# A linear-attention block: denominators and reciprocals per block of rows, placed between the later Q blocks

## The chip, the cores and the metric

One core of a Trainium2 chip (trn2). The metric is the device time of one execution in microseconds (us), median of several runs. Each trace is one profiled execution. A run is called slow when it is over 1.5% above the fastest run of the same kernel.

Terms: TensorE does the matmuls and leaves their results in buffers of PSUM; VectorE and ScalarE read them there, and a buffer is free for the next matmul only when they have. The clock is the share of its full rate that TensorE was granted, as the profile records it; where it falls below 1.00 I say that it is cut.

## The reference, cut to what matters

```python
B, S, D = 1, 2048, 640                      # H = 32 heads of 20
q, k, v = split(x @ wqkv)                   # per head
pq, pk = phi(q), phi(k)                     # phi(t) = (t + 1 if t > 0 else exp(t)) + 1e-6
kv  = einsum("bhsd,bhse->bhde", pk, v)      # needs all rows of k and v
z   = einsum("bhsd->bhd", pk)
num = einsum("bhqd,bhde->bhqe", pq, kv)
den = einsum("bhqd,bhd->bhq", pq, z)[..., None] + 1e-6
out = (num / den) reshaped to (B, S, D) @ wo
```

The kernel folds `kv` and `wo` into one 640 x 640 matrix `gw`, so that each row of output is (pq x 1/den) @ gw. The 2048 rows go in four blocks of 512.

## The kernel before: the parts in question

```python
psum  = tile_pool("ps_main", bufs=5)   # tag "pp": five PSUM buffers for nearly everything
ps_pd = tile_pool("ps_pd", bufs=1)     # the denominator alone
ps128 = tile_pool("ps_128", bufs=2)    # transposes

setup_masks(); q_block(0)
for st in range(16): kv_tile(st)
for sb in (1, 2, 3): q_block(sb, act_relu=True)     # exp, relu on ScalarE; add on VectorE
# ... KV sums: 5 bands of 16 matmuls into g (masked kv) and zspad (z in four shifted copies)

pd = ps_pd.tile([P, 512])                           # 4 blocks x 32 heads = 128 rows
for qq in range(4):
    for k in range(5): matmul(pd, lhsT=zspad[:, k, qq], rhs=pq[:, k, block qq], ...)
nc.vector.reciprocal(rden, pd)                      # one, 128 x 512
# ... 13 transposes of g (copied out by ScalarE), 26 fold matmuls -> gw

for qq in range(4):                                 # expansion of 1/den and multiply
    for mi in range(5):
        pr = psum.tile(tag="pp")
        matmul(pr, lhsT=epad[:, qq, mi], rhs=rden)
        nc.vector.tensor_tensor(pqs[:, mi, block qq], pq[:, mi, block qq], pr, mult)
for st in range(16):                                # output
    po0, po1 = psum.tile(), psum.tile()
    # ... 5 + 5 matmuls of pqs with gw; ScalarE casts po0, VectorE casts po1, then the store
```

Of the kernel before, what the change touches and what calls it, by code (L numbers as in the profile page):

```python
# [13 lines left out]
def kernel(  # L14
# [7 lines left out]
    nc = tc.nc  # L22
    P = nc.NUM_PARTITIONS
    B, S, D = x.shape
    assert B == 1
    H = 32
    Dh = D // H
    KT = D // P
    assert D == P * KT and H * Dh == D
    NS = S // P  # L30
    SB = 512
    NSB = S // SB
    NQ = S // 512
    assert S % 512 == 0 and NQ <= 4

    bf16 = mybir.dt.bfloat16
    f32 = mybir.dt.float32
# [15 lines left out]
    bands = []  # L53
    for mi in range(KT):
        hlo = (mi * P) // Dh
        hhi = (mi * P + P - 1) // Dh
        c0 = hlo * Dh
        c1 = (hhi + 1) * Dh
# [18 lines left out]
    gt_pairs = []  # L77
    pair_idx = {}
    for kt in range(KT):
        hlo, hhi, c0, c1, _, _, _ = bands[kt]  # L80
# [5 lines left out]
    work = ctx.enter_context(tc.tile_pool(name="work", bufs=3))  # L86
# [3 lines left out]
    wo_sb = consts.tile([P, KT, D], bf16, name="wo_sb")  # L90
# [4 lines left out]
    ident = consts.tile([P, P], bf16, name="ident")  # L95
# [4 lines left out]
    g = consts.tile([P, KT, D], bf16, name="gmat")  # L100
    gt = consts.tile([P, len(gt_pairs), P], bf16, name="gtmat")
    zspad = consts.tile([P, KT, NQ, P], bf16, name="zspad")
    gw = consts.tile([P, KT, D], bf16, name="gw")
# [11 lines left out]
    for oc in ONE_COLS:  # L115
# [5 lines left out]
        out=ident[:],  # L121
        in_=ident[:],
# [6 lines left out]
    for qq in range(NQ):  # L129
        nc.gpsimd.memset(epad[:, qq, :], 1.0)  # L130
        nc.gpsimd.affine_select(
            out=epad[:, qq, :],
            in_=epad[:, qq, :],
# [7 lines left out]
            out=epad[:, qq, :],  # L141
            in_=epad[:, qq, :],
# [8 lines left out]

    with ExitStack() as p1:
        psum = p1.enter_context(tc.tile_pool(name="ps_main", bufs=5, space=bass.MemoryType.PSUM))
        ps_pd = p1.enter_context(tc.tile_pool(name="ps_pd", bufs=1, space=bass.MemoryType.PSUM))
        ps128 = p1.enter_context(tc.tile_pool(name="ps_128", bufs=2, space=bass.MemoryType.PSUM))

        def setup_masks():
# [12 lines left out]
        def evict_q(pt, out_ap):  # L170
            e = work.tile([P, 512], bf16, name="phi_e")
            r = work.tile([P, 512], bf16, name="phi_r")
            nc.scalar.activation(out=e[:, :], in_=pt[:, :], func=AF.Exp)
            nc.vector.tensor_scalar(
                out=r[:, :], in0=pt[:, :], scalar1=0.0, scalar2=EPS, op0=ALU.max, op1=ALU.add
            )
            nc.vector.scalar_tensor_tensor(
                out=out_ap, in0=e[:, :], scalar=1.0, in1=r[:, :], op0=ALU.min, op1=ALU.add
            )

        def evict_q_act(pt, out_ap):
            e = work.tile([P, 512], bf16, name="phi_e")
            r = work.tile([P, 512], bf16, name="phi_r")
            nc.scalar.activation(out=e[:, :], in_=pt[:, :], func=AF.Exp)  # L184
            nc.scalar.activation(out=r[:, :], in_=pt[:, :], func=AF.Relu, bias=epst[:], scale=1.0)  # L185
            nc.vector.scalar_tensor_tensor(  # L186
                out=out_ap, in0=e[:, :], scalar=1.0, in1=r[:, :], op0=ALU.min, op1=ALU.add
            )

        def q_block(sb, act_relu=False):  # L190
            for mi in range(KT):
                pt = psum.tile([P, 512], f32, name="pp", tag="pp")
                for k in range(KT):
                    nc.tensor.matmul(  # L194
                        pt[:, :],
                        lhsT=w_sb[:, k, bass.ts(mi, P)],
                        rhs=xt[:, k, bass.ts(sb, SB)],
                        start=(k == 0),
                        stop=(k == KT - 1),
                    )  # L200
                if act_relu:
                    evict_q_act(pt, pq[:, mi, bass.ts(sb, SB)])
                else:
                    evict_q(pt, pq[:, mi, bass.ts(sb, SB)])
# [56 lines left out]
        q_block(0)  # L261
        for st in range(NS):
            kv_tile(st)
        for sb in range(1, NSB):
            q_block(sb, act_relu=True)

        for mi in range(KT):
            hlo, hhi, c0, c1, b0, b1, zcol = bands[mi]
            W = b1 - b0
            pb = psum.tile([P, 512], f32, name="pp", tag="pp")  # L270
            for st in range(NS):
                nc.tensor.matmul(  # L272
                    pb[:, 0:W],
                    lhsT=pk[:, st, bass.ts(mi, P)],
                    rhs=va[:, st, b0:b1],
                    start=(st == 0),
                    stop=(st == NS - 1),
# [8 lines left out]
            for s0_, s1_ in segs:  # L286
# [3 lines left out]
                    out=g[:, mi, s0_:s1_],  # L290
# [6 lines left out]
                out=zspad[:, mi, 0, 0:H], in0=et[:, mi, :], scalar1=pb[:, zoff : zoff + 1]  # L297
# [1 line left out]
            for qq in range(1, NQ):  # L299
                nc.scalar.copy(out=zspad[:, mi, qq, 32 * qq : 32 * qq + H], in_=zspad[:, mi, 0, 0:H])  # L300

        pd = ps_pd.tile([P, 512], f32, name="pd", tag="pd")
        for qq in range(NQ):
            for k in range(KT):
                nc.tensor.matmul(  # L305
                    pd[:, :],
                    lhsT=zspad[:, k, qq, :],
                    rhs=pq[:, k, qq * 512 : (qq + 1) * 512],
                    start=(qq == 0 and k == 0),
                    stop=(qq == NQ - 1 and k == KT - 1),  # L310
                )
        rden = work.tile([P, 512], bf16, name="rden", bufs=1)
        npd = NQ * 32
        if npd < P:
            nc.vector.memzero(rden[:])
        with nc.allow_low_precision("bf16 reciprocal of den is fine"):
            nc.vector.reciprocal(rden[:npd, :], pd[:npd, :])

        for pi, (kt, nt) in enumerate(gt_pairs):
            ptp = ps128.tile([P, P], bf16, name="ptp", tag="t128")  # L320
            nc.tensor.transpose(ptp[:, :], g[:, kt, bass.ts(nt, P)], ident[:, :])
            nc.scalar.copy(out=gt[:, pi, :], in_=ptp[:, :])

        for kt in range(KT):
            hlo, hhi, c0, c1, _, _, _ = bands[kt]
            nts = list(range(c0 // P, (c1 - 1) // P + 1))
            HD = D // 2
            gw0 = psum.tile([P, 512], f32, name="pp", tag="pp")
            gw1 = psum.tile([P, 512], f32, name="pp", tag="pp")
            for i, nt in enumerate(nts):  # L330
                nc.tensor.matmul(  # L331
                    gw0[:, :HD],
                    lhsT=gt[:, pair_idx[(kt, nt)], :],
                    rhs=wo_sb[:, nt, 0:HD],
                    start=(i == 0),
                    stop=(i == len(nts) - 1),
                )
                nc.tensor.matmul(  # L338
                    gw1[:, :HD],
                    lhsT=gt[:, pair_idx[(kt, nt)], :],  # L340
                    rhs=wo_sb[:, nt, HD:D],
                    start=(i == 0),
                    stop=(i == len(nts) - 1),
                )
            nc.scalar.copy(out=gw[:, kt, 0:HD], in_=gw0[:, :HD])
            nc.vector.tensor_copy(out=gw[:, kt, HD:D], in_=gw1[:, :HD])

        for qq in range(NQ):
            for mi in range(KT):
                pr = psum.tile([P, 512], f32, name="pp", tag="pp")  # L350
                nc.tensor.matmul(  # L351
                    pr[:, :],
                    lhsT=epad[:, qq, bass.ts(mi, P)],
                    rhs=rden[:, :],
                    start=True,
                    stop=True,
                )
                nc.vector.tensor_tensor(  # L358
                    out=pqs[:, mi, qq * 512 : (qq + 1) * 512],
                    in0=pq[:, mi, qq * 512 : (qq + 1) * 512],  # L360
                    in1=pr[:, :],
                    op=ALU.mult,
                )

        HD = D // 2
        for st in range(NS):
            po0 = psum.tile([P, 512], f32, name="pp", tag="pp")
            po1 = psum.tile([P, 512], f32, name="pp", tag="pp")
            for k in range(KT):
                nc.tensor.matmul(  # L370
                    po0[:, :HD],
                    lhsT=pqs[:, k, bass.ts(st, P)],
                    rhs=gw[:, k, 0:HD],
                    start=(k == 0),
                    stop=(k == KT - 1),
                )
                nc.tensor.matmul(  # L377
                    po1[:, :HD],
                    lhsT=pqs[:, k, bass.ts(st, P)],
                    rhs=gw[:, k, HD:D],  # L380
                    start=(k == 0),
                    stop=(k == KT - 1),
                )
            ob = work.tile([P, D], bf16, name="ob")
            nc.scalar.copy(out=ob[:, 0:HD], in_=po0[:, :HD])  # L385
            nc.vector.tensor_copy(out=ob[:, HD:D], in_=po1[:, :HD])  # L386
            nc.sync.dma_start(out2[bass.ts(st, P), :], ob[:, :])


# [28 lines left out]
```

## Time and profile before

| | before |
|---|---|
| median at the prediction | 130.36 us (6 runs) |
| span of the profiled execution | 127.5 us |
| K/V stage ends | 60.2 us |
| last output matmul ends | 124.1 us |
| between the two ("the stretch") | 63.9 us |
| TensorE's own work in the stretch | 56.7 us |

The change touches only the stretch. I read its ends from TensorE's instructions in order of time: the end of the last K/V matmul and the end of the last output matmul. It doesn't depend on how fast the inputs arrived. The prediction shows the lines.

### The profile page before, as it was taken

What the parts mean: (1) busy time and instruction counts of PE and PEld (TensorE: products, weight loads), DVE (VectorE), ACT (ScalarE), POOL (GpSimd) and SP (SyncE); (2) the same over time, 40 slices, a digit from 0 to 9 for tenths busy, and PEclk for the clock granted to TensorE, in tenths of its full rate; (3) what the DMA queues carried; (4) which work ended last, traced back from release to release, by engine and by line L of the source; (5) the groups of instructions that cost most, each with busy time, mean ns of one, the idle gap of its engine ahead of it and who ended that gap; (6) DMA issues with size and microseconds to landing.
All of it is one profiled execution on the core that took longest, in us unless ns stands there. A gap on an engine that the chain in (4) does not pass through costs nothing.

```text
span 127.5 us, 1909 instructions
## 1 busy us (share of the span) xinstructions
PE 117.0 (92%) x674; PEld 63.1 (49%) x674; DVE 71.0 (56%) x133; ACT 66.5 (52%) x212; POOL 8.4 (7%) x18
## 2 busy tenths in 40 slices
PE   0769999999999999999999999999968999999990
PEld 0414445455445555455444449746511267777760
DVE  5306984444555554444666667409899964334331
ACT  4556355566666655566999996408500013233230
POOL 8980000000000000000000000000000000000000
PEclk9999999999999999999999999999996579999999
DMA  2989999900000000000000000000000004223422
GB/s 54 247 268 343 343 209 194 198 3 0 0 0 0 0 3 5 0 0 0 0 0 3 5 0 0 0 0 5 0 0 0 0 0 149 108 105 114 147 105 101
DMA packets 14776, 8.63 MB, mean 68 GB/s; under 512 B 10800, under 2 KB 14128, under 8 KB 14768
## 3 DMA queue, kind: packets, MB, share of 16 engines
q1 hardware_dynamic: 14768, 8.52, 23.9%
q8 instruction: 5, 0.08, 0.3%
q14 instruction: 3, 0.02, 0.1%
HBM read 3.28 MB, written 2.62 MB: 46 GB/s over the span
## 4 chain that ended last, share of the span: by engine, by line
PE 82%; DVE 5%; SPq 4%; DMA 3%; ACT 2%; issue 2%; DVEq 0%; ACTq 0%
PE pp L194 16%; PE pp L211 12%; PE pp L218 12%; PE pp L370 9%; PE pp L377 9%; PE pp L225 8%; PE pp L272 4%; DVE pqs L358 4%; PE pp L351 4%; PE pd L305 3%; DMA wqkv_sb<-in_wqkv_dram 3%; SPq L107 2%; PE pp L338 1%; SPq L109 1%; PE pp L331 1%
## 5 line engine op out<-in xcount | busy, mean ns | idle before, releaser
L211 PE MATMUL pp<-wqkv_sb,xt 128*128 128x512 bf16 x80 | 30.3, 379 | 0.0
L218 PE MATMUL pp<-wqkv_sb,xt 128*128 128x512 bf16 x80 | 30.3, 379 | 0.0
L194 PE MATMUL pp<-xt,wqkv_sb 128*128 128x512 bf16 x100 | 22.9, 385 | 1.0 <-DMA wqkv_sb<-in_wqkv_dram 1.0
L235 DVE TENSOR_SCALAR phi_r<-pp 128x512 bf16<-128x512 f32 x16 | 11.1, 692 | 21.2 <-ACT phi_e L234 21.2
L370 PE MATMUL pp<-gw,pqs 128*128 128x320 bf16 x80 | 21.9, 309 | 0.0
L377 PE MATMUL pp<-gw,pqs 128*128 128x320 bf16 x80 | 21.6, 305 | 0.0
L385 ACT CAST ob<-pp 128x320 bf16<-128x320 f32 x16 | 6.8, 426 | 26.2 <-PE pp L370 24.8
L225 PE MATMUL pp<-wqkv_sb,xt 128*128 128x256 bf16 x80 | 19.3, 271 | 0.2
L234 ACT ACTIVATE phi_e<-pp 128x512 bf16<-128x512 f32 x16 | 9.6, 597 | 18.0 <-PE pp L211 16.9
L194 PEld LDWEIGHTS <-wqkv_sb 128*128 128x128 bf16 x100 | 9.7, 99 | 13.3 <-DMA wqkv_sb<-in_wqkv_dram 2.7
L386 DVE CAST ob<-pp 128x320 bf16<-128x320 f32 x16 | 7.9, 491 | 13.3 <-PE pp L377 12.1
L186 DVE SCALAR_TENSOR_TENSOR pq<-phi_e,phi_r 128x512 bf16<-128x512 bf16 x15 | 10.4, 693 | 5.7 <-ACT phi_r L185 5.6
L225 PEld LDWEIGHTS <-xt 128*128 128x128 bf16 x80 | 7.8, 97 | 10.5 <-issue 4.4
L211 PEld LDWEIGHTS <-xt 128*128 128x128 bf16 x80 | 7.8, 98 | 9.4
L185 ACT ACTIVATE phi_r<-pp,epst 128x512 bf16<-128x512 f32 x15 | 12.4, 823 | 0.0
L358 DVE TENSOR_TENSOR pqs<-pq,pp 128x512 bf16<-128x512 bf16 x20 | 12.0, 683 | 0.0
L184 ACT ACTIVATE phi_e<-pp 128x512 bf16<-128x512 f32 x15 | 11.0, 731 | 0.0
L238 DVE SCALAR_TENSOR_TENSOR pk<-phi_e,phi_r 128x512 bf16<-128x512 bf16 x16 | 10.9, 684 | 0.0
L351 PE MATMUL pp<-rden,epad 128*128 128x512 bf16 x20 | 8.6, 460 | 1.6 <-DVE pqs L358 1.6
L370 PEld LDWEIGHTS <-pqs 128*128 128x128 bf16 x80 | 8.0, 100 | 4.2 <-issue 1.0
L377 PEld LDWEIGHTS <-pqs 128*128 128x128 bf16 x80 | 8.0, 101 | 3.4
L218 PEld LDWEIGHTS <-xt 128*128 128x128 bf16 x80 | 7.8, 97 | 2.6
(51 smaller groups left out, 119.7 us busy)
## 6 DMA issues: line engine op xcount, KB each, us to landing
out_dram<-ob SPq DMA_DIRECT2D x16, 160.0 KB, 1.8
wqkv_sb<-in_wqkv_dram SPq DMA_DIRECT2D x5, 320.0 KB, 5.8
wqkv_sb<-in_wqkv_dram SPq DMA_DIRECT2D x5, 160.0 KB, 2.9
wo_sb<-in_wo_dram SPq DMA_DIRECT2D x1, 800.0 KB, 8.3
xt<-in_x_dram SPq DMA_TRANSPOSE x4, 6.6
```

The source lines that it names most:

```text
L184: nc.scalar.activation(out=e[:, :], in_=pt[:, :], func=AF.Exp)
L185: nc.scalar.activation(out=r[:, :], in_=pt[:, :], func=AF.Relu, bias=epst[:], scale=1.0)
L194: nc.tensor.matmul(pt[:, :], lhsT=w_sb[:, k, bass.ts(mi, P)], rhs=xt[:, k, bass.ts(sb, SB)], start=(k == 0), stop=(k == KT - 1),)
L211: nc.tensor.matmul(g0[:, :], lhsT=xt[:, k, bass.ts(st, P)], rhs=w_sb[:, k, D : D + 512], start=(k == 0), stop=(k == KT - 1),)
L218: nc.tensor.matmul(g1[:, :], lhsT=xt[:, k, bass.ts(st, P)], rhs=w_sb[:, k, D + 512 : D + 1024], start=(k == 0), stop=(k == KT - 1),)
L225: nc.tensor.matmul(g2[:, :256], lhsT=xt[:, k, bass.ts(st, P)], rhs=w_sb[:, k, D + 1024 : 3 * D], start=(k == 0), stop=(k == KT - 1),)
L235: nc.vector.tensor_scalar(out=r0[:, :], in0=g0[:, :], scalar1=0.0, scalar2=EPS, op0=ALU.max, op1=ALU.add)
L238: nc.vector.scalar_tensor_tensor(out=pk[:, st, 0:512], in0=e0[:, :], scalar=1.0, in1=r0[:, :], op0=ALU.min, op1=ALU.add)
L351: nc.tensor.matmul(pr[:, :], lhsT=epad[:, qq, bass.ts(mi, P)], rhs=rden[:, :], start=True, stop=True,)
L358: nc.vector.tensor_tensor(out=pqs[:, mi, qq * 512 : (qq + 1) * 512], in0=pq[:, mi, qq * 512 : (qq + 1) * 512], in1=pr[:, :], op=ALU.mult,)
L370: nc.tensor.matmul(po0[:, :HD], lhsT=pqs[:, k, bass.ts(st, P)], rhs=gw[:, k, 0:HD], start=(k == 0), stop=(k == KT - 1),)
L377: nc.tensor.matmul(po1[:, :HD], lhsT=pqs[:, k, bass.ts(st, P)], rhs=gw[:, k, HD:D], start=(k == 0), stop=(k == KT - 1),)
```

## The change

Intent: VectorE is idle for much of the Q stages, and TensorE waits for VectorE afterwards. So each block gets a denominator and a reciprocal of its own, those of the early blocks start while later Q blocks are computed, and the fold and the first output tiles move between the rest.

```diff
-        ps_pd = p1.enter_context(tc.tile_pool(name="ps_pd", bufs=1, ...))
...
-        for sb in range(1, NSB):
-            q_block(sb, act_relu=True)
+        if NSB > 1:
+            q_block(1, act_relu=True)
... (KV sums as before)
+        rden = work.tile([P, 512], bf16, name="rden", bufs=1)
+        nc.vector.memzero(rden[:])
+        def den_recip(qq):
+            pdq = psum.tile([P, 512], f32, name="pp", tag="pp")
+            ... 5 matmuls
+            nc.vector.reciprocal(rden[32 * qq : 32 * qq + H, :], pdq[32 * qq : 32 * qq + H, :])
...
+        den_recip(0); den_recip(1)
+        ... transposes
+        q_block(2, act_relu=True)
+        den_recip(2)
+        gw_build()
+        q_block(3, act_relu=True)
+        expand_mult(0); expand_mult(1); expand_mult(2)
+        den_recip(3)
+        for st in range(0, 4): out_tile(st)
+        expand_mult(3)
+        for st in range(4, NS): out_tile(st)
```

(The last lines are drawn together and the guards for other sizes left out.)

More of the change, by code (lines that the diff above doesn't have):

```diff
@@ L153 @@
         psum = p1.enter_context(tc.tile_pool(name="ps_main", bufs=5, space=bass.MemoryType.PSUM))
-        ps_pd = p1.enter_context(tc.tile_pool(name="ps_pd", bufs=1, space=bass.MemoryType.PSUM))
         ps128 = p1.enter_context(tc.tile_pool(name="ps_128", bufs=2, space=bass.MemoryType.PSUM))
@@ L300 @@
                 nc.scalar.copy(out=zspad[:, mi, qq, 32 * qq : 32 * qq + H], in_=zspad[:, mi, 0, 0:H])
-        pd = ps_pd.tile([P, 512], f32, name="pd", tag="pd")
-        for qq in range(NQ):
+        rden = work.tile([P, 512], bf16, name="rden", bufs=1)
+        nc.vector.memzero(rden[:])
+        def den_recip(qq):
+            pdq = psum.tile([P, 512], f32, name="pp", tag="pp")
             for k in range(KT):
                 nc.tensor.matmul(
-                    pd[:, :],
+                    pdq[:, :],
@@ L307 @@
                     lhsT=zspad[:, k, qq, :],
                     rhs=pq[:, k, qq * 512 : (qq + 1) * 512],
-                    start=(qq == 0 and k == 0),
-                    stop=(qq == NQ - 1 and k == KT - 1),
-                )
-        rden = work.tile([P, 512], bf16, name="rden", bufs=1)
-        npd = NQ * 32
-        if npd < P:
-            nc.vector.memzero(rden[:])
-        with nc.allow_low_precision("bf16 reciprocal of den is fine"):
-            nc.vector.reciprocal(rden[:npd, :], pd[:npd, :])
@@ L319 @@
-        for pi, (kt, nt) in enumerate(gt_pairs):
-            ptp = ps128.tile([P, P], bf16, name="ptp", tag="t128")
-            nc.tensor.transpose(ptp[:, :], g[:, kt, bass.ts(nt, P)], ident[:, :])
-            nc.scalar.copy(out=gt[:, pi, :], in_=ptp[:, :])
-        for kt in range(KT):
-            hlo, hhi, c0, c1, _, _, _ = bands[kt]
-            nts = list(range(c0 // P, (c1 - 1) // P + 1))
-            HD = D // 2
-            gw0 = psum.tile([P, 512], f32, name="pp", tag="pp")
-            gw1 = psum.tile([P, 512], f32, name="pp", tag="pp")
-            for i, nt in enumerate(nts):
-                nc.tensor.matmul(
-                    gw0[:, :HD],
-                    lhsT=gt[:, pair_idx[(kt, nt)], :],
-                    rhs=wo_sb[:, nt, 0:HD],
-                    start=(i == 0),
-                    stop=(i == len(nts) - 1),
-                )
-                nc.tensor.matmul(
-                    gw1[:, :HD],
-                    lhsT=gt[:, pair_idx[(kt, nt)], :],
-                    rhs=wo_sb[:, nt, HD:D],
-                    start=(i == 0),
-                    stop=(i == len(nts) - 1),
-                )
-            nc.scalar.copy(out=gw[:, kt, 0:HD], in_=gw0[:, :HD])
-            nc.vector.tensor_copy(out=gw[:, kt, HD:D], in_=gw1[:, :HD])
@@ L348, with expand_mult @@
-        for qq in range(NQ):
+                    start=(k == 0),
+                    stop=(k == KT - 1),
+                )
+            with nc.allow_low_precision("bf16 reciprocal of den is fine"):
+                nc.vector.reciprocal(rden[32 * qq : 32 * qq + H, :], pdq[32 * qq : 32 * qq + H, :])
+        def expand_mult(qq):
             for mi in range(KT):
@@ L363, with out_tile @@
                 )
-        HD = D // 2
-        for st in range(NS):
+        def out_tile(st):
             po0 = psum.tile([P, 512], f32, name="pp", tag="pp")
@@ L387, with gw_build @@
             nc.sync.dma_start(out2[bass.ts(st, P), :], ob[:, :])
+        def gw_build():
+            for kt in range(KT):
+                hlo, hhi, c0, c1, _, _, _ = bands[kt]
+                nts = list(range(c0 // P, (c1 - 1) // P + 1))
+                gw0 = psum.tile([P, 512], f32, name="pp", tag="pp")
+                gw1 = psum.tile([P, 512], f32, name="pp", tag="pp")
+                for i, nt in enumerate(nts):
+                    nc.tensor.matmul(
+                        gw0[:, :HD],
+                        lhsT=gt[:, pair_idx[(kt, nt)], :],
+                        rhs=wo_sb[:, nt, 0:HD],
+                        start=(i == 0),
+                        stop=(i == len(nts) - 1),
+                    )
+                    nc.tensor.matmul(
+                        gw1[:, :HD],
+                        lhsT=gt[:, pair_idx[(kt, nt)], :],
+                        rhs=wo_sb[:, nt, HD:D],
+                        start=(i == 0),
+                        stop=(i == len(nts) - 1),
+                    )
+                nc.scalar.copy(out=gw[:, kt, 0:HD], in_=gw0[:, :HD])
+                nc.vector.tensor_copy(out=gw[:, kt, HD:D], in_=gw1[:, :HD])
+        HD = D // 2
+        if NQ >= 2:
+            den_recip(0)
+            den_recip(1)
+        else:
+            for qq in range(NQ):
+                den_recip(qq)
+        for pi, (kt, nt) in enumerate(gt_pairs):
+            ptp = ps128.tile([P, P], bf16, name="ptp", tag="t128")
+            nc.tensor.transpose(ptp[:, :], g[:, kt, bass.ts(nt, P)], ident[:, :])
+            nc.scalar.copy(out=gt[:, pi, :], in_=ptp[:, :])
+        if NSB > 2:
+            q_block(2, act_relu=True)
+        if NQ >= 3:
+            den_recip(2)
+        gw_build()
+        if NSB > 3:
+            for sb in range(3, NSB):
+                q_block(sb, act_relu=True)
+        expand_mult(0)
+        if NQ >= 2:
+            expand_mult(1)
+        if NQ >= 3:
+            expand_mult(2)
+            den_recip(3)
+        for st in range(0, min(4, NS)):
+            out_tile(st)
+        if NQ >= 4:
+            expand_mult(3)
+        for st in range(min(4, NS), NS):
+            out_tile(st)
 _INS = ['x', 'wqkv', 'wo']
```

## The prediction

> **What bounds the kernel now.** I read the page's busy shares and the slices first, then the chain that ended last, then a table of stretches cut where the program changes stage, then VectorE's and TensorE's instructions in order of time around the one stretch that stood out.
>
> The page says that TensorE is the bound, and that VectorE and ScalarE are each busy about half of the span:
>
> ```profile
> PE 117.0 (92%) x674; PEld 63.1 (49%) x674; DVE 71.0 (56%) x133; ACT 66.5 (52%) x212; POOL 8.4 (7%) x18
> PE   0769999999999999999999999999968999999990
> DVE  5306984444555554444666667409899964334331
> ACT  4556355566666655566999996408500013233230
> PEclk9999999999999999999999999999996579999999
> PE 82%; DVE 5%; SPq 4%; DMA 3%; ACT 2%; issue 2%; DVEq 0%; ACTq 0%
> ```
>
> The reader is to see the hole at slices 29 to 33 of 40 (3.19 us each, so about 92 to 105 us): there VectorE is full and the granted TensorE clock falls to half. The change touches nothing before 60.2 us, where the K/V tiles end. The stretches after it (start:end, length, then busy time of PE, PEld, DVE, ACT, POOL, then clock):
>
> ```profile
> 60.20:76.40 16.20, 16.20 (x79) 7.42 (x77) 10.50 (x16) 16.20 (x35) 0.00 (x0) 1.00 0.01 2
> 76.40:81.40 5.00, 5.00 (x81) 5.00 (x79) 3.24 (x12) 2.95 (x15) 0.00 (x0) 1.00 0.00 0
> 81.40:85.70 4.30, 4.30 (x23) 1.94 (x21) 0.45 (x2) 0.60 (x5) 0.00 (x0) 1.00 0.00 0
> 85.70:91.00 5.30, 4.99 (x41) 3.26 (x40) 4.95 (x5) 4.16 (x17) 0.00 (x0) 1.00 0.01 3
> 91.00:101.30 10.30, 8.64 (x22) 1.98 (x21) 10.17 (x19) 0.43 (x1) 0.00 (x0) 0.77 0.00 0
> 101.30:103.60 2.30, 2.30 (x11) 1.33 (x11) 2.30 (x4) 0.43 (x1) 0.00 (x0) 0.57 0.00 0
> 103.60:124.20 20.60, 20.54 (x152) 14.58 (x149) 7.37 (x16) 6.09 (x15) 0.00 (x0) 1.00 0.31 112
> ```
>
> In order: 15 Q tiles, the KV sums, the denominator, transposes and Wo fold, the expansion of 1/den with its multiply, and the output. Two rows show what sets the hole, and one the price of a reciprocal:
>
> ```profile
> 91.56 12.04 DVE L358 TENSOR_TENSOR pqs<-pq,pp 128x512 bf16<-128x512 bf16 x20
> 93.49 0.38 PE L351 MATMUL pp<-rden,epad 128*128 128x512 bf16 x1 [0.22 <-DVE pqs L358]
> 85.86 3.36 DVE L317 RECIPROCAL rden<-pd 128x512 bf16<-128x512 f32 x1 [3.87 <-PE pd L305]
> ```
>
> Twenty multiplies run back to back at 12.04/20 = 0.602 us; each frees one of five PSUM buffers, and the next expansion matmul waits for it. A full-clock 128x512 matmul takes 1.08/5 = 0.216 us (a Q tile of five starts every 16.2/15 = 1.08 us), so TensorE works 36% of that time, and its clock is cut.
>
> **What the Trainium skill says.** "VectorE: DVE Perf Modes", section on why a reduction can't go along partitions: VectorE streams along the free dimension and each partition is its own lane. So a reciprocal of 32 partitions x 512 should cost what the one of 128 x 512 costs. The trace has only the 128-partition one, 3.36 us; no run yet shows the narrow one. "TensorE: Matmul & The Clock Gate", Part 1: a hardware monitor halves the array's clock when it has been too idle, and gives it back after a few us of sustained work. The trace agrees: clock 1.00 up to 96 us, 0.50 from 97 to 103, 1.00 from 104, that is, cut 4 to 5 us after the thin stretch began and returned about 2 us after the output matmuls began. "Perfetto Trace Analysis", Identifying Performance Opportunities: kernels of several regimes can gain by interleaving them (the intent here), and a repeated gap can mean too few PSUM buffers. The 0.22 us wait repeated above is such a gap, though here VectorE's rate is behind it.
>
> **The change part by part.** TensorE's work is the same: 20 denominator, 20 expansion, 26 fold, 160 output matmuls, 13 transposes. From the rows: Q 16.2, KV 5.1, denominator 4.3, transposes and fold 5.0, expansion 20 x 0.216 = 4.3, output 16 tiles x 1.36 = 21.8 us (an output tile starts every 1.36 us after 103.6). Sum 56.7. From 60.2 that would end at 116.9; matmuls now end near 124.1. So 7.2 us is recoverable at most: 10.3 - 4.3 = 6.0 in the expansion, about 1 in output tiles at half clock, the rest small. That is 5.5% of 130.36.
>
> Added: VectorE has four reciprocals of 32 rows in place of one of 128, 3 x 3.36 = +10.1 us, and the denominators now take turns in the same five PSUM buffers (the separate bank is given up, not handed to the pool). Each such buffer is held 3.4 us and more.
>
> Moved: Q blocks 2 and 3 (10 tiles, 10.8 us of TensorE) go behind the first two denominators and around the fold; expansion becomes 15 multiplies, then the last denominator and four output tiles, then 5 multiplies.
>
> A hand schedule, t = 0 at 60.2 us, in the program's order and letting ready work go ahead as the trace of before shows (there transposes and fold matmuls alternate):
> - Q block 1 to 5.4, KV sums to 10.5, denominators 0 and 1 to 12.7. VectorE: two reciprocals, 11.7 to 18.3.
> - Transposes (1.4) and Q block 2 (5.4) to 19.5. ScalarE has 13 copies of 0.26 and 5 tiles of 1.06, 8.7 us, so it ends at 21.7. VectorE's five adds wait for the reciprocals; the exp and relu scratch has three buffers, so ScalarE gets three tiles ahead, just enough.
> - Fold 3.5 and denominator 2 1.1: 24.1 without waits. They are short of PSUM buffers while ScalarE clears Q block 2; I add 0.5, so 24.6. Reciprocal 2 runs 24.0 to 27.4.
> - Q block 3 to 30.0, last add on VectorE near 31.7.
> - Expansion of blocks 0 to 2: the multiplies begin at 30.3 and share VectorE with one add: 30.3 + 15 x 0.602 + 0.6 = 39.9. TensorE may run five ahead, so its last expansion matmul starts near 36.9, where work alone would give 33.2. This is the old hole again, a third shorter: 3.7 us lost.
> - Denominator 3 needs a buffer: 37.5 to 38.6. Reciprocal 3 follows multiply 15: 39.9 to 43.2. Output tiles 0 and 1 fit into the buffers (to 41.4). Tiles 2 and 3 wait, since VectorE's half of each eviction queues behind the reciprocal: they end at 45.0, not 44.1.
> - Expansion of block 3 takes all five buffers, paced by multiplies 45 to 48, so output tile 4 starts near 46.4. Twelve tiles x 1.36 = 16.3, end at 62.7.
>
> Before, the same mark is 124.1 - 60.2 = 63.9. The gain is 1.2 us. If the clock is cut in the thin stretch (30.6 to 37.5, longer than the 4 to 5 us which sufficed before), denominator 3 and a part of output tile 0 run at half speed, and of that delay some 0.7 us survives VectorE's own queue: gain 0.5. I think the cut likely and take 0.7 us.
>
> **The check from VectorE's side.** From 11.7 to the last multiply it has four reciprocals 13.4, ten adds 6.0, five fold casts 2.3, twenty multiplies 12.0, four output casts 1.9: 35.6 us, end at 47.3 without one pause. The schedule has 48. So VectorE, not TensorE, is the bound in that stretch: the change moves the multiplies under nothing (they still stand after the last Q block) and fills the time it opened with reciprocals.
>
> **The rivals.** (1) The interleaving works as meant: multiplies of finished blocks are slipped between Q block 3 matmuls and the hole closes, -4 to -6 us, 124.5 to 126.5. For: VectorE is 56% busy overall. Against: each expansion matmul reads all of the reciprocal tile, so it waits for reciprocal 2 (27.4); Q block 3 stands ahead in the program; the 35.6 us above leave no room. (2) Reciprocals hold VectorE and PSUM buffers so that ScalarE's scratch fills and the Q stages stall: each of three reciprocals may cost 1 us, 131.5 to 133. For: ScalarE is full (16.20 of 16.20) in the Q stage already, with no slack to catch up. Against: three scratch buffers just cover it by my schedule. (3) A narrow reciprocal costs a quarter: then about 10 us leave VectorE and perhaps 3 us the path, 127. Against: lanes are independent.
>
> **Range and chances.** The tail after the last matmul (cast, store, 3.4 us) and everything up to 60.2 stay. The median 130.36 less 0.7 gives 129.7 us. The schedule's slips are of 1 us each and mostly the same sign (waits I did not see), the chance of rivals 1 or 3 pulls the other way: 127.6 to 131.9 for 8 in 10. Faster by over 2% means below 127.75: 0.14. Slower by over 2%, above 132.97: 0.08. Within: 0.78.
>
> **What would show it.** Right if the new profile has four reciprocals near 3.36 us each; VectorE nearly full from about 72 us for some 35 us; the last Q tile ending near 90; a run of 15 multiplies at 0.60 us with TensorE waiting on them, and a clock cut in it; output tiles 2 and 3 delayed by a reciprocal; and 12 output tiles at 1.36 us to the end. Wrong if multiplies lie among Q block 3's matmuls, if the clock stays 1.00 (then 0.7 us better), if TensorE shows waits of over 2 us in Q blocks 2 or 3 (rival 2), or if a reciprocal takes near 1 us (rival 3).

## The result, and the profile after

| | before | changed |
|---|---|---|
| median | 130.37 us (16 runs) | 132.01 us (8 runs) |
| ratio, 95% interval | | 1.0122 (1.0068 to 1.0175) |
| profiled span | 127.5 us | 128.5 us |
| the stretch | 63.9 us | 64.7 us |

All ratios are the mean time of one kernel's fast runs over that of the other's fast runs of the same rounds, so not quite the ratio of the medians. The change makes the kernel about 1% slower. The median, 132.01, lies just above my range (127.6 to 131.9), and I had called a small gain.

First the page of the changed kernel: busy shares, then tenths in 40 slices (3.21 us each).

```profile
PE 116.5 (91%) x674; PEld 62.6 (49%) x674; DVE 80.6 (63%) x137; ACT 66.7 (52%) x212; POOL 8.4 (7%) x18
PE   0769999999999999999999999999759988999990
DVE  5306984444555544445676699997899996734331
...
PEclk9999999999999999999999999999995999999998
L315 DVE RECIPROCAL rden<-pp 32x512 bf16<-32x512 f32 x4 | 13.4, 3353 | 0.8 <-PE pp L307 0.6
```

VectorE went from 71.0 to 80.6 us, nearly the +10.1 us of three more reciprocals. The last row gives their price: 3353 ns each on 32 rows, where the wide one on 128 rows took 3358. TensorE's row still has its hole, only earlier, and a second, shallower one behind it.

The changed kernel's stretch in stages, in the same columns as in the prediction (start:end, length, then busy time of PE, PEld, DVE, ACT, POOL, then clock):

```profile
60.50:90.85 30.35, 30.16 (x209) 17.07 (x208) 24.61 (x36) 23.10 (x68) 0.00 (x0) 1.00 0.01 1
90.85:99.10 8.25, 5.87 (x16) 1.48 (x15) 7.92 (x14) 1.38 (x3) 0.00 (x0) 0.86 0.00 0
99.10:100.67 1.57, 1.57 (x5) 0.60 (x5) 1.57 (x3) 0.00 (x0) 0.00 (x0) 0.67 0.00 0
100.67:106.77 6.10, 5.72 (x41) 3.90 (x40) 5.42 (x6) 1.27 (x3) 0.00 (x0) 1.00 0.07 25
106.77:108.74 1.97, 1.40 (x7) 0.49 (x5) 1.55 (x3) 0.42 (x1) 0.00 (x0) 1.00 0.48 172
108.74:125.10 16.36, 16.36 (x121) 11.64 (x119) 7.24 (x15) 4.68 (x11) 0.00 (x0) 1.00 0.31 111
```

The stages are: everything up to the last Q matmul; 15 expansions; denominator 3; output tiles 0 to 3; block 3's expansion; twelve output tiles. At full clock TensorE would need 29.5, 3.2, 1.1, 5.4, 1.1 and 16.3 us. So 0.9, 5.0, 0.5, 0.7, 0.9 and 0.1 us are lost: 8.0 in all, of which 5.5 lie between the last Q matmul and the first output matmul. In the kernel before it was 7.2 (63.9 - 56.7).

What fills VectorE then, in order of time, in the changed kernel (start, length, instruction):

```profile
91.79 0.68 DVE L327 TENSOR_TENSOR pqs<-pq,pp 128x512 bf16<-128x512 bf16 x1
92.39 0.68 DVE L185 SCALAR_TENSOR_TENSOR pq<-phi_e,phi_r 128x512 bf16<-128x512 bf16 x1
92.99 8.45 DVE L327 TENSOR_TENSOR pqs<-pq,pp 128x512 bf16<-128x512 bf16 x14
101.47 3.36 DVE L315 RECIPROCAL rden<-pp 32x512 bf16<-32x512 f32 x1
104.87 1.29 DVE L354 CAST ob<-pp 128x320 bf16<-128x320 f32 x3
107.19 1.29 DVE L327 TENSOR_TENSOR pqs<-pq,pp 128x512 bf16<-128x512 bf16 x2 [1.03 <-PE pp L320]
```

Fifteen multiplies back to back (with one add of the Q block behind the first), then a reciprocal in front of three output casts, then a wait for block 3's expansion. The old hole is there, with 15 multiplies in place of 20, and behind it a new one.

**Two heaps of runs.** The trace pair says 0.8 us, the medians 1.6. Spans (the experiments' rounds for the kernel before, the result's and the control's for the changed one): those of the kernel before fall into 126.5 to 128.3 us (12 runs, mean 127.7) and 128.7 to 130.2 (17 runs, mean 129.45); those of the changed kernel into 128.4 to 128.5 (3 runs, mean 128.5) and 130.0 to 131.7 (12 runs, mean 130.55). Heap against heap, the change costs 0.7 to 1.1 us. The rest of the 1.6 is that more of its runs lie in the upper heap. Three experiments' profiles (the four casts, the first three casts, the half-width reciprocals) have a late head: in them the K/V stage ends at 61.8 to 62.2 us, against 60.2 to 60.9 in the other eleven profiles. The chain of waits shows why. First matmuls of the kernel before, then of the run with four casts (start, length, line, count):

```profile
9.47 0.82 PE pp L194 x3
```

```profile
9.24 1.89 PE pp L193 x4
```

They start at about the same time but take 0.47 us each, not 0.27: the array begins at half clock and gets the full one later. (The clock records begin, at 1.00, at 12.6 to 13.2 us in these three traces and at 7.3 to 9.0 us in the others.) That is a matter of the head, before anything that the change touches. That the upper heaps are runs with such a head is likely, not shown: no trace of a run in the upper heap of either kernel was kept.

### The profile page after: what moved, and what is told of

It reads as the page before. It is cut to its first block, busy times and chain, and to the rows that moved or that the text cites.

```text
span 128.5 us, 1911 instructions
## 1 busy us (share of the span) xinstructions
PE 116.5 (91%) x674; PEld 62.6 (49%) x674; DVE 80.6 (63%) x137; ACT 66.7 (52%) x212; POOL 8.4 (7%) x18
## 4 chain that ended last, share of the span: by engine, by line
PE 76%; DVE 9%; ACT 4%; DMA 3%; SPq 3%; issue 3%; DVEq 0%; ACTq 0%
PE pp L193 13%; PE pp L210 12%; PE pp L217 12%; PE pp L338 9%; PE pp L345 8%; PE pp L224 8%; PE pp L307 4%; DVE pqs L327 4%; PE pp L271 4%; DMA wqkv_sb<-in_wqkv_dram 3%; DVE rden L315 3%; PE pp L320 2%; SPq L107 2%; ACT phi_r L184 1%; SPq L109 1%
## 5 line engine op out<-in xcount | busy, mean ns | idle before, releaser
L210 PE MATMUL pp<-wqkv_sb,xt 128*128 128x512 bf16 x80 | 30.3, 379 | 0.0
L217 PE MATMUL pp<-wqkv_sb,xt 128*128 128x512 bf16 x80 | 30.3, 379 | 0.0
L193 PE MATMUL pp<-xt,wqkv_sb 128*128 128x512 bf16 x100 | 24.4, 384 | 1.2 <-DMA wqkv_sb<-in_wqkv_dram 1.1
L338 PE MATMUL pp<-gw,pqs 128*128 128x320 bf16 x80 | 21.3, 299 | 0.4 <-ACT ob L353 0.4
L345 PE MATMUL pp<-gw,pqs 128*128 128x320 bf16 x80 | 21.3, 299 | 0.0
L233 ACT ACTIVATE phi_e<-pp 128x512 bf16<-128x512 f32 x16 | 9.6, 597 | 18.0 <-PE pp L210 16.9
L315 DVE RECIPROCAL rden<-pp 32x512 bf16<-32x512 f32 x4 | 13.4, 3353 | 0.8 <-PE pp L307 0.6
L224 PEld LDWEIGHTS <-xt 128*128 128x128 bf16 x80 | 7.8, 97 | 10.5 <-issue 4.4
L210 PEld LDWEIGHTS <-xt 128*128 128x128 bf16 x80 | 7.8, 98 | 9.5
L184 ACT ACTIVATE phi_r<-pp,epst 128x512 bf16<-128x512 f32 x15 | 11.0, 734 | 0.0
L183 ACT ACTIVATE phi_e<-pp 128x512 bf16<-128x512 f32 x15 | 9.6, 641 | 1.8 <-DVE rden L315 1.3
L320 PE MATMUL pp<-rden,epad 128*128 128x512 bf16 x20 | 7.4, 419 | 2.9 <-DVE pqs L327 2.5
```

Of the source, the lines that this page charges most:

```text
L184: nc.scalar.activation(out=r[:, :], in_=pt[:, :], func=AF.Relu, bias=epst[:], scale=1.0)
L193: nc.tensor.matmul(pt[:, :], lhsT=w_sb[:, k, bass.ts(mi, P)], rhs=xt[:, k, bass.ts(sb, SB)], start=(k == 0), stop=(k == KT - 1),)
L210: nc.tensor.matmul(g0[:, :], lhsT=xt[:, k, bass.ts(st, P)], rhs=w_sb[:, k, D : D + 512], start=(k == 0), stop=(k == KT - 1),)
L217: nc.tensor.matmul(g1[:, :], lhsT=xt[:, k, bass.ts(st, P)], rhs=w_sb[:, k, D + 512 : D + 1024], start=(k == 0), stop=(k == KT - 1),)
L224: nc.tensor.matmul(g2[:, :256], lhsT=xt[:, k, bass.ts(st, P)], rhs=w_sb[:, k, D + 1024 : 3 * D], start=(k == 0), stop=(k == KT - 1),)
L315: nc.vector.reciprocal(rden[32 * qq : 32 * qq + H, :], pdq[32 * qq : 32 * qq + H, :])
```

## The experiments

Twelve runs. The stretch is from the end of the last K/V matmul to the end of the last output matmul, read from the one profile of each run. Two of these profiles fell in slow runs, as marked.

| run | order | reciprocals | median us (runs) | ratio to before (95%) | stretch us |
|---|---|---|---|---|---|
| before | before | one, 128x512 | 130.37 (16) | | 63.9 |
| changed | changed | four, 32x512 | 132.01 (8) | 1.0122 (1.0068 to 1.0175) | 64.7 |
| changed, again | changed | four | 132.02 (6) | 1.0093 (1.0010 to 1.0176) | 64.8 |
| four casts | changed | none (casts) | 129.31 (4) | 0.9854 (0.9749 to 0.9958) | 63.0 (slow run) |
| early expansions | blocks 0, 1 before Q block 3 | four | 130.13 (4) | none given | 63.9 |
| both | the same | none (casts) | 125.62 (4) | 0.9652 (0.9596 to 0.9708) | 60.0 |
| own bank | changed | four, own PSUM bank | 128.95 (6) | 0.9912 (0.9865 to 0.9959) | 63.5 |
| block reciprocals only | before | four | 136.06 (4) | 1.0438 (1.0363 to 1.0512) | 70.4 |
| by tile, full | tile by tile | four, own bank | 128.42 (4) | 0.9831 (0.9741 to 0.9922) | 63.9 (slow run) |
| by tile, half | tile by tile | four, 64x256, own bank | 124.42 (4) | 0.9569 (0.9477 to 0.9661) | 57.8 |
| last cast | changed | 0 to 2 | 129.33 (1) | | 63.6 |
| first casts | changed | 3 only | 130.56 (1) | | 63.3 |
| half | changed | four, 64x256 | 130.42 (1) | | 63.3 |
| output interleaved | before, multiplies among output tiles | one, 128x512 | 123.98 (4) | 0.9585 (0.9467 to 0.9703) | 58.2 |

The theories: **A**, VectorE's reciprocals take what the change gains. **B**, the order: the multiplies still stand together behind the last Q block, whatever the reciprocals cost. **C**, the denominators now share the five PSUM buffers, and that costs.

### Casts in place of the reciprocals

```diff
-                nc.vector.reciprocal(rden[32 * qq : 32 * qq + H, :], pdq[...])
+                nc.vector.tensor_copy(out=rden[32 * qq : 32 * qq + H, :], in_=pdq[...])
```

> The changed kernel with each of its four reciprocals replaced by a plain cast of the same 32x512 buffer (wrong numbers on purpose; about 0.6 to 0.7 us in place of 3.36 us, so some 10.7 us less on VectorE). Theory A, the reciprocals on VectorE are what keeps the change from paying: the loss in the Q and fold stages (0.85 us), the wait of output tiles 2 and 3 (0.7), and a part of the hole go: 127.5 to 129 us, ratio to the kernel before 0.98 to 0.99. Theory B, the order: 15 of the 20 multiplies still stand behind the last Q block, so the hole of about 8 us between the last Q matmul and denominator 3 stays whatever the reciprocals cost: 130 to 131 us, ratio 1.00 (gain over the changed kernel of 1.5 us at most), with the stretch from the last Q matmul to denominator 3 still 7.5 us or more. Theory C, the shared PSUM buffers: a buffer is held 2.7 us shorter each time, so about as B.

Its output is wrong, which doesn't matter for the time. The stretch is 63.0 us, 1.7 us less than the changed kernel's for 10.7 us less on VectorE. The stretch from the last Q matmul to the first output matmul is 10.0 us (9.7 in the changed kernel). The hole didn't move, and from the last Q matmul to denominator 3 it is 8.1 us, as B says (7.5 or more); but the ratio, 0.985, is the one that A gave (0.98 to 0.99), not B's 1.00. The profile fell in a slow run (late head, and a cut of the clock). The fastest run, with a clock of 1.000, has a span of 125.8 us, some 1.0 us under the profiled 128.1 less the 1.3 of its late head; so without the cut the stretch may be 62.0, and the gain 2.7 us (an estimate; 2.1 us if the changed kernel's own cut is taken out as well, see "Which of the four reciprocals costs"). Either way it is a small part of the 10.7.

### Expansions of blocks 0 and 1 in front of the last Q block

```diff
-        rden = work.tile([P, 512], ...)              # one tile for all blocks
+        rdens = [consts.tile([P, 512], ...) for qq in range(NQ)]
         gw_build()
+        expand_mult(0); expand_mult(1)
         q_block(3, act_relu=True)
-        expand_mult(0); expand_mult(1); expand_mult(2)
+        expand_mult(2)
```

> The changed kernel with a reciprocal tile of its own for each block (so that an expansion waits only for its own block) and with the expansions of blocks 0 and 1 put in front of the last Q block; reciprocals as they are. Theory A: VectorE has 18 us of work for the 19 us between the first reciprocal and the last Q block already, so ten multiplies more (6.0 us) only push the adds of the last Q block back; nothing gained or some lost: 130.5 to 133 us, ratio 1.00 to 1.02. Theory B: the hole behind the last Q block shrinks from 15 to 5 multiplies, 5.5 us lost there becomes under 1: 126.5 to 128.5 us, ratio 0.97 to 0.985.

The stretch is 63.9: 0.8 us won, not the 4 to 5 that B asked for; the median, 130.13, lies just under A's range (130.5 to 133). VectorE in order of time:

```profile
82.91 3.35 DVE L318 RECIPROCAL rden<-pp 32x512 bf16<-32x512 f32 x1
86.30 1.29 DVE L382 CAST gw<-pp 128x320 bf16<-128x320 f32 x3
87.50 6.06 DVE L330 TENSOR_TENSOR pqs<-pq,pp 128x512 bf16<-128x512 bf16 x10
```

Ten multiplies are again a block of 6 us, and the last Q block's matmuls stand behind their expansions: they start at 91.2 us, not at 85.2. The hole has been moved in front of that Q block.

### Both edits

> Both edits: casts for the reciprocals (wrong numbers on purpose) and the early expansions. Theories A and B both expect the hole to close here: 125 to 127 us, ratio 0.96 to 0.975, no run of more than five multiplies behind the last Q block and no cut of the clock. If A is right this gains far more than the two single edits together; if B is right, little more than the early expansion alone. If neither gains, the cause is elsewhere.

60.0 us: 4.7 less than the changed kernel, where the two edits alone gave 1.7 and 0.8. The clock is not cut here, but that accounts for 0.5 to 0.9 us at most (see "Which of the four reciprocals costs"). So they help each other, as A expects. It is not all: 60.0 is still 3.3 above TensorE's own 56.7.

### Denominators in a PSUM bank of their own

```diff
+        ps_pd = p1.enter_context(tc.tile_pool(name="ps_pd", bufs=1, ...))
-            pdq = psum.tile([P, 512], f32, name="pp", tag="pp")
+            pdq = ps_pd.tile([P, 512], f32, name="pd", tag="pd")
```

> The changed kernel with the denominators in a PSUM bank of their own again (one buffer, as the kernel before had), reciprocals and order as changed. Theory C, sharing the five buffers costs: the 5 us of reciprocals that sit on a buffer no longer hold back Q tiles, fold and output tiles: 1 us or more faster than the changed kernel, ratio 1.00 or below. Theories A and B: within 0.5 us of the changed kernel, ratio 1.005 to 1.017; it may even cost a little, since denominator 1 must wait for reciprocal 0.

C is right here, though not by the way I wrote down. The stretch is 63.5 us, 1.2 less, and the ratio 0.991: with this one bank the change would have been a small gain (0.4 us in the stretch). TensorE in order of time:

```profile
90.55 1.03 PE L321 MATMUL pp<-rden,epad 128*128 128x512 bf16 x4
91.41 0.59 PE L308 MATMUL pd<-pq,zspad 128*128 128x512 bf16 x2
91.97 0.62 PE L321 MATMUL pp<-rden,epad 128*128 128x512 bf16 x2
92.43 0.81 PE L308 MATMUL pd<-pq,zspad 128*128 128x512 bf16 x3
```

Denominator 3's matmuls (L308) need no shared buffer, so they go in among the first expansions. In the changed kernel they came after the fifteenth, at 99.10, mostly at half clock. The first output matmul starts 38.3 us after the K/V stage, not 40.2. The clock row has no cut in this profile before the last output matmul, so about 0.5 of the 1.2 us is that denominator 3 doesn't run at half clock (1.57 us in the changed kernel, 1.08 at full clock). A rival is that the bank only happened to meet a run without a cut. The six runs answer it: three with a mean clock of 0.986 to 0.987 have spans of 127.1 to 127.5 us, three with 0.997 to 1.000 have 127.0 to 127.3. With or without a cut they lie 0.9 to 1.5 us under the changed kernel's fastest (128.4 to 128.5). The medians differ by more, 3.1 us, since none of the six lies in an upper heap; why none does is not shown.

### The control

> The changed kernel once more, unaltered, as a control. In the profiles the stretch from the last K/V matmul to the last output matmul, which the change alone touches, took 63.9 us in the kernel before and 64.7 us in the changed one; the single runs of both kernels fall in two heaps about 1.5 us apart, and one profile with a late head shows the first Q matmuls at half clock. Theory H, the heaps come from the head: like for like the change costs 0.8 us, and a new draw of runs gives a ratio of 1.003 to 1.010. Theory N, nothing of it is chance: the ratio is again 1.010 to 1.015.

64.8 us, and a ratio of 1.0093. That is in H's range, but the interval (1.0010 to 1.0176) covers N's as well, so this run doesn't part them; what it shows is that the stretch repeats within 0.1 us, and that "about 1% slower" stands.

### Block reciprocals alone, in the old order

> One part of the change alone: the kernel before in its old order, with a denominator and a narrow reciprocal of each block (in the shared buffers) in place of the one wide reciprocal. If a narrow reciprocal costs as much as a wide one and all lie on VectorE's way, the first starts about 1.0 us after the first denominator's matmuls, four of 3.36 us end some 13.4 us later, where the single one ended 3.4 us after four denominators (3.2 us later than one): 13.4 - 6.6 = 6.8 us at most, less what hides under transposes and fold: 3.5 to 6 us slower, 134 to 136.5 us, ratio 1.03 to 1.05. If VectorE's free time in the fold hides them: under 1 us slower, ratio below 1.01.

```profile
83.29 13.51 DVE L314 RECIPROCAL rden<-pp 32x512 bf16<-32x512 f32 x4 [0.63 <-PE pp L306]
96.83 2.08 DVE L343 CAST gw<-pp 128x320 bf16<-128x320 f32 x5
98.83 12.04 DVE L355 TENSOR_TENSOR pqs<-pq,pp 128x512 bf16<-128x512 bf16 x20
```

The stretch is 70.4 us: this part of the change costs 6.5 us in the profiles, somewhat over the 3.5 to 6 expected, and 5.4 us between the medians of the same rounds (136.06 and 130.68). The profile has two cuts of the clock (from 93.3 and from 106.9 us), which may hold a part of the 6.5. The rest of the change, the new order, brings the stretch back to 64.7, so it is worth 5.7. Nearly all that the interleaving hides is the work that the change itself added.

### Tile by tile, with full and with half reciprocals

```diff
         for mi in range(KT):
+            q_tile(2, mi)
+            if mi: expand(0, mi - 1)
...
         for mi in range(KT):
+            q_tile(3, mi); expand(1, mi)
         den_recip(3)
         for mi in range(KT):
+            out_tile(mi); expand(2, mi)        # then block 3 among tiles 6 to 10
```

The half version lays a block's denominators out as 64 rows x 256 columns, with the shifted copies of z and of the masks that are there:

```diff
-    matmul(pdq[:, :], lhsT=zspad[:, k, qq, :], rhs=pq[:, k, 512 columns])
+    for j in range(2):
+        matmul(pdq[:, :], lhsT=zspad[:, k, j, :], rhs=pq[:, k, columns of half j])
-    reciprocal(rdens[qq][32 * qq : 32 * qq + H, :], ...)      # 32 x 512
+    reciprocal(rdens[qq][0 : 2 * H, :], ...)                  # 64 x 256
```

> Four reciprocals of 32x512 as in the changed kernel, a reciprocal tile of its own for each block, denominators in their own bank, and the expansions slipped in tile by tile: block 0 among the Q tiles of block 2, block 1 among those of block 3, blocks 2 and 3 one multiply per output tile. Theory A, the reciprocals' 13.4 us of VectorE are the bound: from the last K/V matmul to the last output matmul 62 to 64 us, total 128 to 130 us. Theory B, the order is: VectorE has 41 us of work for the 45 us that TensorE needs from there, so with the right order it all hides: 58 to 60.5 us, total 124.5 to 126.5 us, ratio 0.955 to 0.97, no cut of the clock behind the Q stage.

> The same order with the denominators of a block laid out as 64 rows x 256 columns (two matmuls of 256 columns for one of 512), so that a reciprocal should cost half, 1.7 us; right results. Theory A: most of the gain comes with this, 58 to 59.5 us from the last K/V to the last output matmul, 124 to 126 us in all, 3 us or more better than the same order with full reciprocals. Theory B: at most 1 us better than that one.

The two profiles, 63.9 and 57.8 us, are not of the same state: the full version's fell in a slow run, with the clock at half for a while in the last Q block (0.74 and 0.83 in two stretches of 4 us; its span is 127.9, that of its fast runs 125.8). So I compare the fast runs: spans of 125.8, 125.9 and 127.5 against 121.8, 121.8, 123.6 and 123.6, 3.7 us between the means, and 4.0 between the medians of all runs, for 6.4 us less on VectorE. B falls in the form that I gave it ("with the right order it all hides", at most 1 us between the two). In this order A is right. Two of the full version's lines on VectorE, two on TensorE, and the half version's reciprocals:

```profile
85.65 3.35 DVE L322 RECIPROCAL rden<-pd 32x512 bf16<-32x512 f32 x1
89.02 2.08 DVE L389 CAST gw<-pp 128x320 bf16<-128x320 f32 x5
```

```profile
88.07 0.43 PE L381 MATMUL pp<-wo_sb,gtmat 128*128 128x320 bf16 x2 [0.51 <-ACT gw L388]
89.56 0.38 PE L326 MATMUL pp<-rden,epad 128*128 128x512 bf16 x1 [1.06 <-DVE gw L389]
```

```profile
L323 DVE RECIPROCAL rden<-pd x4: 1742/1749/1750, 72.6 to 95.3; 64x256 bf16<-64x256 f32 x4
```

A reciprocal is one instruction of 3.35 us (here 85.65 to 89.0). All five of the fold's casts on VectorE stand behind it, their PSUM buffers stay full, and TensorE's next expansion waits 1.06 us for the last of them. A sum of work doesn't see that.

### Which of the four reciprocals costs

> The changed kernel with only the reciprocal of block 3 replaced by a cast (wrong numbers on purpose), read from the trace: the stretch from the last K/V matmul to the last output matmul, 64.7 us in the changed kernel, 63.0 with all four cast. The prediction held that reciprocals 0 to 2 hide and that reciprocal 3 delays output tiles 2 and 3 by 0.9 us and block 3's multiplies behind them. If so: 63.5 to 63.9 us here. If the last reciprocal hides too: 64.4 or more.

> The counterpart: reciprocals 0 to 2 replaced by casts (wrong numbers on purpose), block 3's kept. If they hide nearly wholly in the Q and fold stages: 63.8 to 64.4 us for the same stretch, with the last Q matmul ending 29.6 to 30.2 us after the last K/V matmul, not 30.5. If they are what holds the multiplies back: 63.0 to 63.4 us and the first multiply over 1 us earlier.

> The changed order with right results and reciprocals of 64 x 256 (1.75 us each in the run before, four for 7.0 us in place of 13.4), and a reciprocal tile of its own per block. If the reciprocals cost by their length on VectorE, their price in this order, 1.7 us for 10.6 us, comes down in proportion: 63.4 to 64.2 us for the stretch. If what counts is that the order leaves 15 multiplies behind the last Q block, the hole from the last Q matmul to the first output matmul stays at 9 us or more (9.7 in the changed kernel, 10.0 with casts), and the total stays above 127 us.

Without the last, 63.6 (-1.1): as the prediction held, it delays the output casts and block 3. Without the first three, 63.3 (-1.4): more than I expected, though the last Q matmul ends 29.6 us after the K/V stage in place of 30.5, as forecast. The two add to 2.5 us, more than the 1.7 of all four casts. Denominator 3 shows why, first in the changed kernel, then with four casts, then with the first three casts:

```profile
99.10 1.73 PE L307 MATMUL pp<-pq,zspad 128*128 128x512 bf16 x5
```

```profile
99.53 2.12 PE L307 MATMUL pp<-pq,zspad 128*128 128x512 bf16 x5
```

```profile
99.88 1.24 PE L307 MATMUL pp<-pq,zspad 128*128 128x512 bf16 x5 [0.22 <-DVE pqs L330]
```

It starts 38.6, 37.7 and 37.7 us after the K/V stage, and the first output matmul follows 1.57, 1.95 and 1.08 us later: the cut of the clock covers part of it, all of it, and none. From there to the end of the stretch it is 24.5 us with the last reciprocal (changed, first casts) and 23.3 without (four casts, last cast). So in this order reciprocals 0 to 2 cost 0.9 us and reciprocal 3 costs 1.2, together 2.1 of their 10.7; what is left over between these profiles is the clock. In the 14 clock records every cut before the last output matmul begins a whole number of 3.41 us steps after the record's start and lasts one or two of them (3.41 or 6.83 us), so it can meet the same matmuls in one run and miss them in another.

Half reciprocals in the changed order: 63.3, with 9.8 us from the last Q to the first output matmul. Reciprocals at half price help little where the multiplies still stand together.

### The old kernel, with multiplies among the output tiles

```diff
-        for qq in range(NQ):            # all 20 expansions
-            for mi in range(KT): ...
-        for st in range(NS): ...        # all 16 output tiles
+        for mi in range(KT): expand(0, mi)
+        for st in range(NS):
+            out_tile(st)
+            # then two expansions of blocks 1 to 3 after tiles 0 to 2, one after each later one
```

> The kernel before with its one wide reciprocal and its Q stages untouched; only the 15 multiplies of blocks 1 to 3 are slipped among the output tiles, one or two per tile. An output tile gives VectorE 0.49 us of work per 1.36 us of TensorE, so one multiply of 0.60 fits under it. Left open is block 0: about 0.6 + 5 x 0.60 = 3.6 us for 1.1 us of matmuls. Sum: 30.8 us to the fold's end, 3.6, then 16 x 1.36 + 15 x 0.216 = 25.0: 59.4; I expect 59.3 to 60.5 us for the stretch (63.9 before), 125.5 to 127.5 us in all, ratio 0.96 to 0.98. If it stays near 64, then the hole was not the multiplies standing together.

58.2 us and 123.98 us, ratio 0.9585, right results: faster than I expected, and 8 us below the changed kernel; its four runs (123.80 to 124.09) all lie below every run of the kernel before. Its page, and VectorE in order of time:

```profile
PE   0797999999999999999999999999998999999990
DVE  5303985555554444444566666840789996677531
...
PEclk9999999999999999999999999999999999999998
```

```profile
92.08 3.66 DVE L357 TENSOR_TENSOR pqs<-pq,pp 128x512 bf16<-128x512 bf16 x6
95.69 0.49 DVE L386 CAST ob<-pp 128x320 bf16<-128x320 f32 x1
96.09 0.68 DVE L357 TENSOR_TENSOR pqs<-pq,pp 128x512 bf16<-128x512 bf16 x1
```

Six multiplies, then cast and multiply in turn. The hole is gone, the clock is not cut before the last output matmul, and the one wide reciprocal lies under the fold as it did. This version and "by tile, half" both beat both kernels; their intervals overlap, and the output version is the smaller edit by far.

## Why the prediction was wrong

By its own steps.

- **Right: what bounds the stage.** VectorE is the bound behind the last Q block, the 15 multiplies stand there at 0.60 us each, the clock is cut among them, and the last reciprocal delays output tiles 2 and 3. All are in the lines above. Narrow reciprocals cost 3.35 us, so rival 3 fell; no multiply lies among the last Q block's matmuls, so rival 1 fell. Rival 2 gave 131.5 to 133 us and the median lies there, but its mechanism came true only in part: TensorE shows no wait of 2 us in Q blocks 2 and 3, and 0.9 us is lost up to the last Q matmul, where rival 2 had up to 3 and the schedule 0.5.
- **Wrong: the size of what stays open behind the last Q block, and with it the sign.** The hand schedule put the end of the stretch at 62.7 us; it was 64.7. Term by term, counted from the end of the K/V stage (60.48 us in that trace): denominator 3 starts at 38.6 (schedule 37.5, +1.1) and takes 1.57 us (schedule 1.1, +0.5). From output tile 0 to output tile 4 it is 108.74 - 100.67 = 8.1 (schedule 46.4 - 38.6 = 7.8, +0.3). The last twelve tiles are within 0.2. That is the 2.0, the roundings aside.
- The +1.1 is the step "the multiplies begin at 30.3 ... and share VectorE with one add". The last Q matmul ends at 30.5 (schedule 30.0), and two adds stand in the way, not one: the first multiply starts at 31.3, behind the Q block's fourth add, and the fifth add follows it. Multiply 15 ends at 41.0 (schedule 39.9), and denominator 3 behind the expansions is as late. With casts for reciprocals 0 to 2 the first multiply starts at 30.4 and denominator 3 at 37.7, so these reciprocals hide less than the schedule assumed.
- The +0.5 is the cut of the clock, for which the prediction had set 0.7 us aside: the forecast, 0.7 us of gain, means a stretch of 63.2, and the miss is 1.5. This mechanism was right.
- The own-bank run shows what denominator 3's place hangs on: it needs a shared buffer only because the change gave its bank up. I had noted that ("given up, not handed to the pool") and had it stand there in the schedule ("needs a buffer: 37.5 to 38.6"), but I priced the shared buffers at 0.5 us in the fold alone. The bank is worth 1.2 us, and most of it at another place: the first output matmul comes 1.9 us earlier with it, of which 0.35 is won before the last Q matmul ends, and 0.65 is lost again after that output matmul.
- The +0.3 is the step "expansion of block 3 takes all five buffers, paced by multiplies 45 to 48". They ran from 46.7 to 50.2, since their matmuls came only after output tile 3 was complete, and VectorE stood idle 1.03 us before them.
- **The baseline.** I compared with one profile of the kernel before, in which the clock was cut for over 6 us, and took its 63.9 as typical. The heaps show the profiled before to be a middling run of its lower heap (126.5 to 128.3), the profiled changed kernel near its fastest. So even a right schedule would have been too kind to the change by some tenths. How much of the 1.6 us between the medians is a chance share of the upper heap stays open: 12 of 15 runs of the changed kernel lie there, 17 of 29 of the kernel before.
- **The check from VectorE's side** was the better guide in its words, though not in its sum (end at 47.3; the last multiply ended at 50.2): "fills the time it opened with reciprocals" is what the block-reciprocals run shows, +6.5 us for the part and -5.7 for the order. I should have asked what the interleaving would be worth without its own additions. The answer was already in the columns of the profile before: 160 output matmuls with VectorE 36% busy, right behind the hole.

## What to carry to other kernels

Before moving work under another stage, ask how much of it the move itself creates: here three added reciprocals and a PSUM bank given up ate all of the gain; a reciprocal costs by its columns, not its rows. Interleave single instructions of the engine that is short with tiles of a stage in which it is idle; whole blocks only move the hole. When buffers are regrouped, ask which matmul could have run in the hole and no longer can.

## What the Trainium skill lacked or had wrong

- "VectorE: DVE Perf Modes" tells how a reciprocal is computed (section "First, the fixed hardware budget"), but gives no time for one. The runs show 3.35 us for 32 x 512, 3.36 for 128 x 512 and 1.75 for 64 x 256: about 6.3 ns per column ((3353 - 1749) / 256) whatever the rows, several times a multiply of the same columns (0.60 us). Its statement that each partition is its own lane agrees with this.
- "TensorE: Matmul & The Clock Gate", section "Why this matters for your kernels", gives as a practical rule to leave no idle gap of TensorE above some 3 us. In the kernel before the clock was halved at 96 us with no gap near that: one matmul of 0.38 us every 0.60 us, with waits of 0.22, was thin enough. (Its section on PSUM-queue cycling does name short idle times between groups as a cause, without a number for how thin is too thin. An estimate from the start times of the matmuls, 0.216 us for 512 columns: in each of the nine 3.41 us steps at full clock that ended in a cut TensorE had worked 23 to 37% of the step; of all other such steps in the stretches the thinnest were 37% (first casts) and 38% (early expansions), and those were not followed by one.) The same page's half and full clock (0.50 and 1.00) are what all profiles show.
- "Perfetto Trace Analysis", section "Optimization Strategy", advises to interleave regimes, but not at which grain. Here interleaving by blocks gave 64.7 us for the stretch (63.9 without it), interleaving by tiles 57.8 and 58.2 (with half-width reciprocals, and with the one wide one). The grain alone is not enough: by tiles with four full reciprocals it was 63.9, in a slow run.
